# Block sums of the second weights from SBUF, and one load of values per chunk

## The chip, the cores and the metric

The kernel runs on one core of a Trainium2 chip. The metric is the device time of one execution in microseconds, from a few executions of the same program; the profiled execution is one more, and its span (first to last instruction) is what the rows of the trace are measured in.

## The reference

Three parts follow each other: local attention, a first feed-forward part with a layer norm, and a second, wider feed-forward part. All of it is float32, and the first two weight matrices and the two of the second part come in as 64-bit floats.

```
for each chunk of 32 tokens (B=4, H=8, S=768, D=64):        # attention
    keys, values = 8 memory rows + tokens from 16 before the chunk to 8 after it
    out = softmax(q @ keys.T / 8) @ values
x = out as [3072, 512]
h = x @ moe_w_in [512, 1024]; s = h * softmax(h)            # first part
x = ((s - mean) / sqrt(var + 1e-6) * g_ln) @ moe_w_out [1024, 512]
h = x @ moe2_w_in [512, 2048]                               # second part
out = (h * clip(h + 3, 0, 6) / 6) @ moe2_w_out [2048, 512]
```

## The kernel before

The 3072 tokens are 24 tiles of 128. The kernel is written as lists of names, and the order of the names is the order of the instructions on each engine; no scheduler moves them. `FIRST` is the way in (tiles 0 to 8 of the attention, the conversion of the first part's weights). `BODY` is one step of a loop over m = 8 to 23 and handles several tiles at once at different depths: it loads q, k and v for tiles m+6, m+7 and m+3, makes scores for m+3, applies probabilities to values for m+1 (`v_p`), multiplies by moe_w_in for m (`m1`), and by moe_w_out for a pair of earlier tiles (`m2`). m = 7 is written out at the end of `FIRST` (entries with @). `LAST` is the way into the second part; after it come only that part's products. "Step m" below is the pass of `BODY` for that m.

While the steps run, two more things are done beside them, for use in the second part. First, the 32 blocks of moe2 weights (16 of moe2_w_in, 16 of moe2_w_out, two in each step) are turned from 64-bit into 32-bit floats. The line of work for one block is: `load_w2` (SyncE, a transfer of 512 KB into z0 or z1, L431 and L434), `w2_abs` (ScalarE, L309), `w2_hold` (GpSimd, L316), `w2_bits` 0, 1, 2 (VectorE, L320, L323, L326), and `w2_store` (SyncE, to w2d in DRAM, L449). A z tile holds one block, so the next load of its kind can start only when `w2_bits` 2 has read it. Secondly, the second part multiplies by blocks in a scheme with fewer products, for which it needs sums and differences of blocks. For these `load_pair` (L852) reads two stored blocks back from DRAM into `pair`, `sum_pair` makes four block sums of 128x256 on GpSimd (L859, L861), and `sums_out` (L872) stores them.

```
def load_pair(kind, j):
    raw["pair"] = T("xal", [P, 2, 2, 256], name="pair")
    SP.dma_start(out=raw["pair"], in_=w2d[kind][j]...)
```

Every transfer of the loop is issued by SyncE (SP in the rows, SPq where its queue waits), in the order of the lists. `load_v` issues 8 loads a tile (4 chunks by 2 groups of 4 heads, L278); for the first two tiles of each batch, which are loaded in steps 9, 10, 15 and 16, it issues 8 more for the memory rows (L274).

A PSUM bank named h is shared: `m1` fills it, `ln_max` (DVE L710), `ln_exp` (ACT L716) and `ln_solu` (DVE L727) read it, then `qk_go` (PE L547) takes it for transposes of q and k, ScalarE copies those out to kT and qc (L303), and only then can the next `m1` (PE L701) write it. On ScalarE these copies stand around `w2_abs`, on VectorE `ln_max` and `ln_solu` stand among the `w2_bits`.

Of the kernel before, what the change touches and what calls it, by code (L numbers as in the profile page):

```python
# [61 lines left out]
    wo_bits:3,0 wo_hi:4 wo_lo:1 wo_bits:3,1 wo_hi:2 m2:0,3 wo_lo:2 ln_sq:3 wo_bits:3,2 wo_hi:5 m1:5,0 ln_var:3
    wo_hi:3 s_max:7 m2:0,0 wo_lo:4 wo_lo:5 wo_lo:3 m2:0,1 q_e:8,0,A ln_pow:3 wo_bits:7,2 x_h:6,1 ln_norm:3 ln_p:3,1
    ln_sq:4 ln_p:3,0 m2:0,4 load_w2:0 k_e:8,1,D wo_hi:7 ln_max:5 wo_lo:7 q_e:8,1,A load_w2:1 wo_hi:6 wo_lo:6 s_sub:7
    ln_exp:5 x_l:6,1 m2:0,2 s_exp:7 w2_abs:1,A m2:0,5 m1:6,0 w2_abs:0,A ln_den:5 ln_solu:5 m2_e:0,0 w2_hold:1,D
    ln_mean:5 ln_h:3,1,0 ln_sq:5 ln_var:4 ln_h:3,0,1 ln_l:3,0,1 s_sum:7 ln_var:5 ln_pow:5 w2_bits:1,0 s_rec:7
    s_norm:7,D ln_l:3,1,0 m1:6,1 m2_e:0,1 ln_norm:5 p_p:7 m2:0,6 p_e:7,0,A ln_pow:4 ln_norm:4 w2_hold:0,D s_p:8
    load_k:10 p_e:7,1,A ln_max:6 ln_exp:6 m2_s:0,0 load_v:7 v_p:7 load_k:9 ln_p:4,1 ln_p:4,0 m2:0,7 w2_bits:1,1
    w2_bits:1,2 x_h:7,0 x_l:7,0 load_w2:3 ln_den:6 m2:0,9 ln_solu:6 ln_mean:6 ln_h:4,1,0 ln_l:4,1,0 w2_store:1
    w2_abs:3,A load_q:9 s_max:8 m2:0,8 m2_s:0,1 ln_sq:6 ln_var:6 s_sub:8 s_exp:8 s_sum:8 m2:0,10 m2:0,11 ln_p:5,0  # L70
    m2_e:0,2 load_v:9 s_rec:8 ln_h:4,0,0 load_q:10 ln_pow:6 m2_s:0,2 ln_l:4,0,0 q_p:9 m2_e:0,3 ln_h:5,0,0 ln_l:5,0,0
    q_go:9,A ln_p:5,1 ln_h:5,1,0 s_norm:8,P ln_norm:6 k_mem:9,D block_p:9 load_k:11 load_q:11 block_p:10 block_e:9,A
    block_e:10,A load_k:12 ln_l:5,1,0 @m2:0 late_turn @s_p_at:6 @qk_p_at:6 @k_e_at:6,3 @k_e_at:6,0 @k_e_at:6,1
    @q_e_at:6 @k_e_at:6,2 p_p:8 p_e:8,1,A @m2:2 w2_hold:3,P p_e:8,0,A @s_max @s_sub @s_exp load_q:12 @w2_bits:0,0
    @w2_bits:0,1 @m1:0 @w2_bits:0,2 @w2_store:0 m2_s:0,3 load_k:13 @load_w2:0 @w2_abs:0 @w2_bits:1,0 @w2_bits:1,1
    @w2_bits:1,2 @w2_store:1 @m1:1 @ln_p @load_w2:1 @s_sum @s_norm @ln:max @ln_h:0 @w2_hold:0 @ln:exp @ln:den @v_p
# [11 lines left out]
    ln_l:1 p_e:0  # L88
# [72 lines left out]
def tile_chunked_attention_solu_hardswish(  # L161
# [1343 lines left out]
```

## Time and profile before

| | us |
|---|---|
| median of 3 executions | 897.89 |
| lowest and highest | 896.66 and 899.6 |
| the profiled execution | 896.33 |
| its span, first to last instruction | 894.5 |

The profiled execution is 1.56 us under the median, and its span 1.83 us under its own time. Busy shares are of the span. TensorE's clock has two levels, 1.2 and 2.4 GHz; the column PEclk gives the granted share of the higher one.

### The profile page before, as it was taken

To read this page: it belongs to the slowest core of one execution; us is meant where nothing else is said; L and a number is where in the kernel's file an instruction comes from. 1 tells how busy PE (TensorE), PEld (TensorE's weight loads), DVE (VectorE), ACT (ScalarE), POOL (GpSimd) and SP (SyncE) were. 2 spreads that over 40 slices of the span, in tenths; PEclk is the share of its full clock that TensorE was granted. 3 is DMA by queue.
4 is the path that set the end of the run, shared out by engine and by line. 5 is a ranking of instruction groups with operands and counts; after the bars stand their busy time and mean duration, and the time that the engine had idled before them with its cause. 6 is when DMAs were issued, how large, how long until landed. Compare 5 with 4: busy or idle time off the path is not lost.

```text
span 894.5 us, 22089 instructions
## 1 busy us (share of the span) xinstructions
PE 856.8 (96%) x8526; PEld 808.1 (90%) x8526; DVE 735.8 (82%) x1510; ACT 478.5 (53%) x946; POOL 252.6 (28%) x226
## 2 busy tenths in 40 slices
PE   9999999988999899998989999999999999999997
PEld 7777887977898789898989999999999999999997
DVE  7889976856687687756588999898899999999985
ACT  5888654645655555444363545545665444444542
POOL 4336214543645556534331111112430000000000
PEclk9999999999999999999999999999999999999999
DMA  8782476768897787654564456354877544444441
GB/s 229 194 267 65 110 181 201 226 186 244 270 242 215 243 229 232 186 177 147 188 209 175 156 198 235 123 211 175 266 259 233 196 153 132 139 156 136 138 142 60
DMA packets 185257, 168.34 MB, mean 188 GB/s; under 512 B 106816, under 2 KB 155456, under 8 KB 185152
## 3 DMA queue, kind: packets, MB, share of 16 engines
q1 hardware_dynamic: 184864, 166.67, 59.9%
q8 instruction: 67, 1.10, 0.5%
q14 instruction: 38, 0.31, 0.1%
q10 hardware_dynamic: 288, 0.26, 0.1%
HBM read 108.17 MB, written 58.72 MB: 187 GB/s over the span
## 4 chain that ended last, share of the span: by engine, by line
PE 65%; DVE 11%; DMA 11%; ACT 4%; issue 4%; SPq 3%; POOL 2%; DVEq 0%; POOLq 0%; ACTq 0%
PE acc L1104 22%; PE acc L1017 20%; PE m L805 8%; PE h L701 7%; DMA w2raw<-in_moe_w_out_dram 3%; DMA w2raw<-in_moe_w_in_dram 3%; PE tp L670 1%; SPq L278 1%; DMA pair<-w2d 1%; DVE f_s L1055 1%; DVE lst L710 1%; PE idle L1172 1%; DMA f_qb<-sums 1%; PE s L540 1%; DMA g<-f_s 1%
## 5 line engine op out<-in xcount | busy, mean ns | idle before, releaser
L805 PE MATMUL m<-lnh,wo 128*128 128x256 f32 (+1 forms) x704 | 144.2, 295 | 2.9 <-DVE x2o L815 2.8
L805 PEld LDWEIGHTS m<-lnh,wo 128*128 128x128 f32 x704 | 114.5, 190 | 5.5 <-DVE x2o L815 3.1
L701 PE MATMUL h<-w,xh 128*128 128x512 f32 x336 | 107.3, 401 | 6.0 <-ACT kT L303 6.0
L1052 ACT ACTIVATE f_s<-f_e,constants 128x512 f32<-128x512 f32 x96 | 67.9, 720 | 81.7 <-DVE f_e L1045 63.8
L805 PE MATMUL m<-lnl,wo 128*128 128x256 f32 (+1 forms) x352 | 102.2, 291 | 0.0
L701 PEld LDWEIGHTS h<-w,xh 128*128 128x128 f32 x336 | 62.0, 190 | 19.4 <-ACT kT L303 7.5
L1055 DVE SCALAR_TENSOR_TENSOR f_s<-f_s,f_e 128x512 f32<-128x512 f32 x96 | 69.9, 736 | 0.9 <-ACT f_s L1052 0.9
L316 POOL TENSOR_SCALAR w2t<-w2t 128x512 f32<-128x512 f32 x30 | 58.4, 1946 | 38.5 <-ACT w2t L309 32.0
L805 PEld LDWEIGHTS m<-lnl,wo 128*128 128x128 f32 x352 | 67.0, 190 | 0.7
L701 PE MATMUL h<-w,xl 128*128 128x512 f32 x168 | 66.2, 394 | 0.3 <-POOL xl L346 0.3
L815 DVE COPY x2o<-m 128x512 f32<-128x512 f32 (+1 forms) x26 | 16.6, 646 | 35.1 <-PE m L805 35.1
L716 ACT ACTIVATE e<-h,lst 128x1024 f32<-128x1024 f32 x24 | 26.8, 1116 | 30.3 <-DVE lst L710 30.3
L906 ACT ACTIVATE b_qb<-f_kn 128x384 fp32r<-128x384 f32 (+1 forms) x48 | 27.7, 577 | 28.2 <-DVE f_kn L1083 15.7
L309 ACT ACTIVATE w2t<-w2raw 128x512 f32<-128x512 f32 x32 | 21.4, 671 | 35.2 <-DMA w2raw<-in_moe_w_in_dram 15.5
L701 PEld LDWEIGHTS h<-w,xl 128*128 128x128 f32 x168 | 32.0, 190 | 7.7 <-POOL xl L346 0.7
L1041 DVE TENSOR_TENSOR f_e<-acc,f_e 128x512 f32<-128x512 f32 x48 | 32.9, 685 | 5.5 <-PE acc L1017 4.5
L346 DVE TENSOR_TENSOR lnl<-tp,lnh 128x512 fp32r<-128x512 f32 x41 | 28.1, 686 | 11.1 <-ACT lnh L342 11.1
L710 DVE TENSOR_REDUCE lst<-h 128x1 f32<-128x1024 f32 x24 | 29.2, 1215 | 7.1 <-PE h L701 7.0
L1049 DVE TENSOR_TENSOR f_e<-acc,f_e 128x512 f32<-128x512 f32 x48 | 32.9, 686 | 1.1 <-PE acc L1017 0.2
L644 POOL TENSOR_TENSOR pn<-pe,ast 128x512 f32<-128x512 f32 x21 | 22.2, 1058 | 36.6 <-DVE ast L640 19.8
L303 ACT ACTIVATE pb<-tp 64x512 f32<-64x512 f32 x47 | 27.9, 593 | 7.7 <-PE tp L652 4.0
L727 DVE SCALAR_TENSOR_TENSOR so<-h,lst,e 128x1024 f32<-128x1024 f32 x24 | 30.8, 1283 | 0.8
(465 smaller groups left out, 2547.9 us busy)
## 6 DMA issues: line engine op xcount, KB each, us to landing
g<-f_s SPq DMA_DIRECT2D x48, 512.0 KB
v<-in_v_dram SPq DMA_DIRECT2D x176, 56.0 KB
w2raw<-in_moe_w_in_dram SPq DMA_DIRECT2D x16, 512.0 KB
w2raw<-in_moe_w_out_dram SPq DMA_DIRECT2D x16, 512.0 KB
w2d<-w2t SPq DMA_DIRECT2D x32, 256.0 KB
pair<-w2d SPq DMA_DIRECT2D x16, 512.0 KB
sums<-sums SPq DMA_DIRECT2D x16, 512.0 KB
q_raw<-in_q_dram SPq DMA_DIRECT2D x24, 256.0 KB
```

The source lines that it names most:

```text
L316: ENG[eng].tensor_scalar(out=tf, in0=tf, scalar1=U_LO, scalar2=U_HI, op0=ALU.max, op1=ALU.min)
L346: (POOL if far else DVE).tensor_tensor(lo, r, hi.bitcast(F32), ALU.subtract)
L701: PE.matmul(h[:, f], a[:, kt], w[kt][:, f * 512:(f + 1) * 512], start=n == 0, stop=n == 3 * NKT - 1)
L710: DVE.tensor_reduce(st_t[i][:, 2:3], h_t[i].rearrange("p a b -> p (a b)"), axis=AX.X, op=ALU.max, negate=True)
L727: DVE.scalar_tensor_tensor(out=so_t[i], in0=h_t.pop(i).rearrange("p a b -> p (a b)"), scalar=st[:, 5:6], in1=e_t[i], op0=ALU.mult, op1=ALU ...
L805: PE.matmul(acc, w[fc // 2][:, fc % 2, dc * P:(dc + 1) * P], a[:, fc], start=fresh and k == 0, stop=k == len(todo) - 1, skip_group_check=True)
L1017: PE.matmul(o, w[wl][:, c * P:(c + 1) * P], x[xl][:, c], start=m == 0 and half == 0, stop=m == 5, skip_group_check=True)
L1041: DVE.tensor_tensor(c_of(n)[1], bank(n % 2, 2), wide(c_of(n)[0][:, 1]), ALU.add)
L1049: DVE.tensor_tensor(c, bank(n % 2, 3), c, ALU.add)
L1052: ACT.activation(out=g_of(n)[k], in_=c_of(n)[k], func=AF.Relu, bias=three, scale=1.0)
L1055: DVE.scalar_tensor_tensor(out=g_of(n)[k], in0=g_of(n)[k], scalar=6.0, in1=c_of(n)[k], op0=ALU.min, op1=ALU.mult)
L1104: PE.matmul(bank(t % 2, k)[:, half], g[al][:, G_BLOCK[p]], b_op[j, p][bl], start=j == 0 and m == 0 and half == 0, stop=j == NU - 1 and m = ...
```

## The change

`load_pair` is gone. The blocks of moe2_w_in now stay in the tile xal (two at a time), those of moe2_w_out in t0 and t1 by block number, and `sum_pair` reads them there, as soon as both of a pair are converted; the sums start at step 7 with moe2_w_out and end at step 22. `w2_store` leaves out the quarter of the blocks' columns that only the sums needed from DRAM (every other store is 256 columns instead of 512). In `BODY`, `sum_pair` moves from the start of the step to behind the last `w2_bits`, and `sums_out` from between the two weight loads to behind both.

`load_v` takes all 8 heads of a chunk in one transfer: 4 loads a tile instead of 8, and 4 for the memory rows instead of 8. The tiles of values and probabilities are laid out to fit, and with them the order in which `s_p`, `s_go`, `p_q` and `v_p` write their blocks and where `s_edge` masks; the number and shapes of their matmuls stay. The lists `FIRST` and `LAST` are written in another order.

```diff
 BODY = """
-    sum_pair m1:1 m1:0 w2_bits:0,0 m2:0 s_max w2_bits:0,1 w2_bits:1,0 s_sub w2_bits:0,2 ln:max w2_bits:1,1 s_exp
-    w2_bits:1,2 m2:1 ln:exp w2_store:0 v_p ln:den ln:solu s_sum s_p load_w2:0 x_h qk_p k_e:0 ln:mean sums_out q_e
-    w2_store:1 k_e:1 w2_abs:0 k_e:3 s_norm k_mem w2_hold:0 ln_p m2:2 m2:3 load_w2:1 ln:sq load_v x_l turn m2_e k_e:2
-    p_p ln:var load_k ln_h:0 load_pair ln:pow ln_l:0 ln_h:1 ln:norm w2_abs:1 p_e:1 m2_s load_q ahead w2_hold:1
+    m1:1 m1:0 w2_bits:0,0 m2:0 s_max w2_bits:0,1 w2_bits:1,0 s_sub w2_bits:0,2 ln:max w2_bits:1,1 s_exp w2_bits:1,2
+    sum_pair m2:1 ln:exp w2_store:0 v_p ln:den ln:solu s_sum s_p load_w2:0 x_h qk_p k_e:0 ln:mean q_e w2_store:1
+    k_e:1 w2_abs:0 k_e:3 s_norm k_mem w2_hold:0 ln_p m2:2 m2:3 load_w2:1 sums_out ln:sq load_v x_l turn m2_e k_e:2
...
     def load_v(i):
...
+        for c in range(4):
+            x, r0 = c % 2, 64 * (c // 2)
+            if i % TPB < 2 and (i >= 2 or x == 0):
+                SP.dma_start(out=dst[r0:r0 + NM, x], in_=mem_v[b].rearrange("h m d -> m h d"))
...
+            SP.dma_start(out=dst[r0 + NM + lo - s0:r0 + NM + hi - s0, x],
+                         in_=v[b, :, lo:hi, :].rearrange("h t d -> t h d"))
...
     def w2_abs(u, eng):
-        raw["w2t", u] = T(f"t{u % 2}", [P, 512], U32, "w2t")
+        f, part = divmod(u, 2)
+        if part:
+            raw["w2t", u] = T(f"t{f % 2}", [P, 512], U32, "w2t")
+        else:
+            if f % 2 == 0:
+                raw["w2p"] = T("xal", [P, 2, 512], U32, "w2t")
+            raw["w2t", u] = raw["w2p"][:, f % 2]
...
     def sum_pair(kind, j):
-        w = raw["pair"]
+        w = [raw["w2t", 4 * j + 2 * f + kind].bitcast(F32).rearrange("p (h c) -> p h c", h=2) for f in range(2)]
...
         def pair_of(m):
-            return 1 - m % 2, (m - 8) // 2
+            return m % 2, (m - STEADY) // 2
```

SyncE, from the first weight load of step 9 on, before (names: w2raw are the 64-bit blocks, w2d and sums_0_139 DRAM, w2t the converted blocks, kn the keys):

```order
L431 DMA w2raw<-in_moe_w_in_dram 128x4x128
L872 DMA sums_0_139<-sums 128x1024
L449 DMA w2d_1_124<-w2t 128x512
L434 DMA w2raw<-in_moe_w_out_dram 128x512
L274 DMA v_134<-in_mem_v_dram 8x4x64 x4
L278 DMA v_134<-in_v_dram 40x4x64
L278 DMA v_134<-in_v_dram 56x4x64 x3
L274 DMA v_134<-in_mem_v_dram 8x4x64 x4
L278 DMA v_134<-in_v_dram 40x4x64
L278 DMA v_134<-in_v_dram 56x4x64 x3
L256 DMA kn_131<-in_k_dram 128x8x64
L852 DMA pair<-w2d_1_124 128x1024
```

The same place of the changed kernel:

```order
L426 DMA w2raw<-in_moe_w_in_dram 128x4x128
L451 DMA w2d_1_124<-w2t 128x512
L429 DMA w2raw<-in_moe_w_out_dram 128x512
L861 DMA sums_1_148<-sums 128x1024
L272 DMA v_134<-in_mem_v_dram 8x8x64
L275 DMA v_134<-in_v_dram 40x8x64
L272 DMA v_134<-in_mem_v_dram 8x8x64
L275 DMA v_134<-in_v_dram 56x8x64
L272 DMA v_134<-in_mem_v_dram 8x8x64
L275 DMA v_134<-in_v_dram 56x8x64
L272 DMA v_134<-in_mem_v_dram 8x8x64
L275 DMA v_134<-in_v_dram 56x8x64
```

The store of the sums has moved behind the second weight load, the sixteen loads of values are eight, and no load of a pair follows the keys.

GpSimd in step 9, with what each instruction waits for in brackets (DMAHW is a transfer's landing), before:

```order
L861 TENSOR_TENSOR sums<-pair 128x256 [waits DMAHW4_49,DMAHW0_49,Pool_49]
L859 TENSOR_TENSOR sums<-sums,pair 128x256 [waits Pool_49]
L859 TENSOR_TENSOR sums<-pair 128x256
L859 TENSOR_TENSOR sums<-pair,sums 128x256 [waits Pool_49]
L644 TENSOR_TENSOR pn<-pe,ast 128x512 [waits DVE_49,PE_49,Activation_49]
L316 TENSOR_SCALAR w2t<-w2t 128x512 [waits DMAHW7_49,Activation_49]
```

And of the changed kernel, where one pair later stands in its place:

```order
L848 TENSOR_TENSOR sums<-w2t 128x256 [waits DMAHW6_49]
L848 TENSOR_TENSOR sums<-w2t,sums 128x256 [waits DVE_49,Pool_49]
L848 TENSOR_TENSOR sums<-w2t 128x256
L848 TENSOR_TENSOR sums<-w2t,sums 128x256 [waits Pool_49]
L642 TENSOR_TENSOR pn<-pe,ast 128x512 [waits DVE_49,PE_49,Activation_49]
L311 TENSOR_SCALAR w2t<-w2t 128x512 [waits Activation_49]
```

The four sums keep their place in GpSimd's order, ahead of the attention's `s_norm` (pn) and the next block's `w2_hold`; what they wait for is VectorE (the last `w2_bits`) instead of the landing of a pair.

## Rows read from the trace of the kernel before

**Rows 1.** The page: span, and busy time of each engine.

```profile
span 894.5 us, 22089 instructions
PE 856.8 (96%) x8526; PEld 808.1 (90%) x8526; DVE 735.8 (82%) x1510; ACT 478.5 (53%) x946; POOL 252.6 (28%) x226
```

**Rows 2.** Busy by stretch, cut where `v_p` starts: length, PE, PEld, DVE, ACT, POOL, PEclk, DMA, GB/s.

```profile
60.00:137.08 77.08, 71.55 (x655) 61.46 (x653) 66.09 (x110) 52.52 (x110) 27.72 (x23) 0.98 0.53 136
137.08:168.59 31.51, 29.52 (x395) 26.39 (x393) 24.63 (x41) 19.27 (x43) 13.60 (x11) 1.00 0.73 208
168.59:183.36 14.77, 14.77 (x205) 13.45 (x204) 10.31 (x21) 7.64 (x17) 8.21 (x8) 1.00 0.57 178
183.36:222.17 38.81, 31.89 (x409) 28.37 (x409) 23.89 (x43) 18.73 (x41) 16.42 (x16) 0.96 0.77 226
222.17:253.78 31.61, 29.75 (x409) 26.78 (x408) 23.78 (x41) 18.39 (x43) 17.82 (x17) 1.00 0.92 263
253.78:283.95 30.17, 29.62 (x409) 26.94 (x409) 21.98 (x44) 16.68 (x37) 16.41 (x16) 1.00 0.73 214
283.95:321.16 37.21, 31.84 (x410) 27.99 (x409) 24.78 (x43) 19.40 (x43) 19.33 (x20) 0.95 0.86 255
321.16:350.87 29.71, 29.48 (x409) 26.75 (x409) 23.84 (x41) 17.32 (x37) 17.21 (x15) 1.00 0.74 223
350.87:379.14 28.27, 27.76 (x313) 25.02 (x312) 21.76 (x38) 13.91 (x28) 17.71 (x18) 1.00 0.65 195
```

**Rows 3.** Timeline, SyncE's queue, step 9 into step 10: start, length, issues.

```profile
173.66 0.42 SPq L434 DMA_DIRECT2D w2raw<-in_moe_w_out_dram  x1
175.65 2.94 SPq L278 DMA_DIRECT2D v<-in_v_dram  x4
...
182.21 0.58 SPq L852 DMA_DIRECT2D pair<-w2d  x1
...
184.81 0.45 SPq L431 DMA_DIRECT2D w2raw<-in_moe_w_in_dram  x1
```

**Rows 4.** Timeline, 181 to 194 us; in brackets the idle time ahead and its releaser.

```profile
181.07 0.43 DVE L320 TENSOR_SCALAR w2t<-w2t 128x512 uint32<-128x512 uint32 x1 [2.14 <-POOL w2t L316]
...
186.93 0.47 PE L547 MATMUL qk<-ident,q_raw 64*128 64x64 f32 x8 [1.62 <-issue]
...
191.22 0.67 ACT L309 ACTIVATE w2t<-w2raw 128x512 f32<-128x512 f32 x1 [2.15 <-DMA w2raw<-in_moe_w_in_dram]
...
193.34 0.73 PE L701 MATMUL h<-w,xh 128*128 128x512 f32 x2 [0.99 <-ACT kT L303]
```

**Rows 5.** Timeline, SyncE's queue around 253.78, where `v_p` of step 14 starts.

```profile
251.30 0.38 SPq L431 DMA_DIRECT2D w2raw<-in_moe_w_in_dram  x1
...
257.61 0.67 SPq L434 DMA_DIRECT2D w2raw<-in_moe_w_out_dram  x1
```

**Rows 6.** Waits of SyncE's queue, whole span: us in total, times, longest.

```profile
SPq L872 <- POOL sums L859: 62.4, 16, 5.3
...
SPq L278 <- DMA w2raw<-in_moe_w_out_dram: 10.0, 13, 1.5
```

**Rows 7.** Timeline around 253.78: the end of the block conversion, `ln_solu`, `qk_go`, `w2_abs`.

```profile
252.93 0.69 DVE L326 SCALAR_TENSOR_TENSOR w2t<-w2raw,w2t 128x512 uint32<-128x512 uint32 x1
...
254.00 1.28 DVE L727 SCALAR_TENSOR_TENSOR so<-h,lst,e 128x1024 f32<-128x1024 f32 x1
...
255.65 0.47 PE L547 MATMUL qk<-ident,q_raw 64*128 64x64 f32 x8
...
257.68 0.67 ACT L309 ACTIVATE w2t<-w2raw 128x512 f32<-128x512 f32 x1
```

**Rows 8.** Timeline around 320 us: VectorE's last `w2_bits`, a block sum on GpSimd.

```profile
320.49 1.11 DVE L326 SCALAR_TENSOR_TENSOR w2t<-w2raw,w2t 128x512 uint32<-128x512 uint32 x1
...
319.87 1.19 POOL L859 TENSOR_TENSOR sums<-pair 128x256 f32<-128x256 f32 x1
```

**Rows 9.** Timeline, TensorE in `LAST`.

```profile
409.30 0.44 PE L805 MATMUL m<-lnh,wo 128*128 128x384 f32 x1 [2.80 <-DVE x2o L815]
```

More of the change, by code (lines that the diff above doesn't have):

```diff
@@ L62 @@
[L62 to L76, printed above, removed]
@@ new lines @@
+    ln_var:5 s_sum:7 s_rec:7 load_w2:0 w2_abs:0,A m2_e:0,0 m1:6,1 ln_var:4 ln_pow:5 ln_norm:5 ln_pow:4 w2_hold:1,D
+    ln_h:3,1,0 s_norm:7,D p_p:7 w2_bits:1,0 load_k:9 ln_norm:4 load_v:7 ln_l:3,1,0 m2:0,6 ln_p:4,1 m2_s:0,0
+    p_e:7,1,A ln_max:6 p_e:7,0,A ln_h:4,1,0 s_p:8 w2_bits:1,1 w2_bits:1,2 v_p:7 x_h:7,0 load_w2:3 load_k:10
+    w2_store:1 ln_p:4,0 ln_l:4,1,0 ln_p:5,0 k_mem:9,D m2:0,7 w2_hold:0,D ln_exp:6 ln_den:6 ln_solu:6 ln_mean:6
+    s_max:8 ln_sq:6 m2:0,8 ln_var:6 x_l:7,0 m2:0,9 m2:0,10 load_q:9 s_sub:8 s_exp:8 m2_e:0,2 ln_h:4,0,0 s_sum:8
@@ L80 @@
+    @w2_store:1 @sum_pair @sums_out @s_sum @s_norm @load_w2:1 @m1:0 @m1:1 @ln:max @w2_abs:0 @ln_p @ln:exp @ln:den
+    @s_p @ln:solu @v_p @x_h @ln:mean @m2:3 @m2:1 @ln_h:0 @ln_l:0 @m2_e @qk_p @p_p @load_q @ln_h:1 @ln_l:1 @k_e:0
+    @k_e:3 @x_l @q_e @k_e:1 @k_e:2 @load_k @k_mem @ln:sq @ln:var @w2_hold:0 @ln:pow @w2_abs:1 @p_e:1 @w2_hold:1
+    @ln:norm @w2_store:0 @p_e:0 @m2_s @load_v
 """
 BODY = """
-    sum_pair m1:1 m1:0 w2_bits:0,0 m2:0 s_max w2_bits:0,1 w2_bits:1,0 s_sub w2_bits:0,2 ln:max w2_bits:1,1 s_exp
@@ L89 @@
+    k_e:1 w2_abs:0 k_e:3 s_norm k_mem w2_hold:0 ln_p m2:2 m2:3 load_w2:1 sums_out ln:sq load_v x_l turn m2_e k_e:2
+    p_p ln:var load_k ln_h:0 ln:pow ln_l:0 ln_h:1 ln:norm w2_abs:1 p_e:1 m2_s load_q ahead w2_hold:1 ln_l:1 p_e:0
 """
@@ L228, in tile_chunked_attention_solu_hardswish @@
     km = [km[:, 0], km[:, 1]]
-    vx = [T(f"v{i}", [P, 4, 4, D]) for i in range(2)]
+    vx = [T(f"v{i}", [P, 2, H, D]) for i in range(2)]
     qb = T("qb", [P, 4, 4, 2, C])
-    pb = T("pb", [P, 4, 4, 2, C])
+    pb = T("pb", [P, 2, H, 2, C])
     kT = [T("kT", [P, 4, 4, NK])] * 2
@@ L448, in w2_store @@
         f, part = divmod(u, 2)
-        SP.dma_start(out=w2d[part][f // 2][:, f % 2], in_=raw["w2t", u].bitcast(F32))
+        kept = slice(0 if f % 2 == part else 256 * (1 - part), 512 if f % 2 == part else 512 - 256 * part)
+        SP.dma_start(out=w2d[part][f // 2][:, f % 2, kept], in_=raw["w2t", u].bitcast(F32)[:, kept])
     def load_g():
@@ L598, in s_edge @@
     def s_edge(i):
-        first, last = (slice(0, C), slice(3 * C, P)) if i >= BLOCKS else (slice(0, P), slice(0, P))
-        if i % TPB == 0:
-            t = sc_t[i][first] if i >= BLOCKS else sc_t[i][:, 0]
-            for t in [t[:, y] for y in range(2)] if i >= BLOCKS else [t]:
-                DVE.memset(t[..., NM:NM + LC], NEG)
-        if i % TPB == TPB - 1:
-            t = sc_t[i][last] if i >= BLOCKS else sc_t[i][:, 3]
-            for t in [t[:, y] for y in range(2)] if i >= BLOCKS else [t]:
-                DVE.memset(t[..., NK - RC:NK], NEG)
+        for edge, n, keys in ((0, 0, slice(NM, NM + LC)), (TPB - 1, 3, slice(NK - RC, NK))):
+            if i % TPB == edge and i >= BLOCKS:
+                for y in range(2):
+                    DVE.memset(sc_t[i][:, y, n, keys], NEG)
+            elif i % TPB == edge:
+                DVE.memset(sc_t[i][:, n // 2, :, n % 2, keys], NEG)
     def s_max(i):
```

203 lines of the change are left out of this document (93 added, 110 removed).

## Prediction

> **What bounds the kernel now.** I began with the page: TensorE is busy for 96% of the span, the next engine, VectorE, for 82% [rows 1]. So the time is TensorE's work plus the places where it stands still or runs at its lower clock, and no stage can give more than those. The view by stretch, cut where `v_p` starts, shows where they are in the loop [rows 2]. The stretch from 168.59 is one step in which TensorE never stops: 14.77 us long, 14.77 busy. I call that a full step. Thirteen of the fifteen steps between 137.08 and 379.14 have the same work; the last two (28.27 together) have less. What each stretch has over full steps (two steps are 29.54):
>
> - 137.08 to 168.59: 31.51, over by 1.97
> - 183.36 to 222.17: 38.81, over by 9.27, at a granted clock of 0.96
> - 222.17 to 253.78: 31.61, over by 2.07
> - 253.78 to 283.95: 30.17, over by 0.63
> - 283.95 to 321.16: 37.21, over by 7.67, at 0.95
> - 321.16 to 350.87: 29.71, over by 0.17
>
> Together 21.8 us. Two stretches have 16.94 of it; they follow steps 9, 10, 15 and 16, in which memory rows are loaded as well. The entries lie at the two ends of this: the stretch from 60 to 137.08, in which TensorE is idle for 77.08 - 71.55 = 5.5, and a stop of 2.80 in `LAST` [rows 2, 9].
>
> Next I asked what TensorE waits for in the first bad stretch, and went back from there. The transposes of q and k start at 186.93 after 1.62 idle, and the next `m1` at 193.34 after 0.99, released by a copy of ScalarE [rows 4]. The first is VectorE's lateness: it had stood 2.14 before 181.07 until GpSimd had held a block [rows 4]. That block's load was issued at 173.66 [rows 3], 7.4 us before. The second is ScalarE, which stood 2.15 before 191.22 for the load of the other block [rows 4], with copies out of bank h queued behind it. That load was issued at 184.81 [rows 3], 1.45 after the cut at 183.36, while in a full step it goes out at 251.30, 2.48 before the cut at 253.78 [rows 5]: 3.9 us late.
>
> Both lates are made in SyncE's queue. After 173.66 it issues sixteen loads of values and one of keys before the pair at 182.21 [rows 3], 18 steps from issue to issue in 8.55 us, 0.475 each. Four of them alone took 2.94 [rows 3], and the waits say why: SyncE stood at these loads 13 times, 10.0 us in all, for the load of moe2_w_out to land [rows 6]. The other wait is `sums_out`: 16 times, 62.4 us [rows 6]. Behind it stands the load of moe2_w_out, which goes out at 257.61 although the block's z tile was free at 252.93 + 0.69 = 253.62 [rows 5, 7]. So a ring runs through the queue: load of a pair, block sums, `sums_out`, weight load, loads of values, next load of a pair.
>
> **The change part by part.**
>
> *The pair's load and the wait for it.* The sums need no transfer any more, and `sums_out` stands behind the weight load. The load of moe2_w_out can then go out at about 253.7 in place of 257.61, 3.9 us earlier; the stop that it ends was 2.14 [rows 4, 5, 7], so it is hidden with 1.8 to spare. `sums_out` still waits for GpSimd, but what stands behind it now (values, keys, x2d, q) is needed a step or more later. That is the edit that I cost at nothing; its cover is the time until the next weight load, some 10 us, and it is gone if values take longer than that.
>
> *Values.* In steps 9, 10, 15 and 16 eight issues fewer: 8 x 0.475 = 3.8 us, about the 3.9 by which 184.81 is late. The bound on the other side: a transfer of twice the bytes takes twice as long to issue, and nothing is saved. I take the first, since the issue waits here for landings of other transfers and not for its own bytes [rows 6]; in the other case the load at 184.81 still gains the pair's 0.58 and the earlier start.
>
> *What this gives in TensorE's time.* The four bad steps take 76.02. I expect them at 14.95, between the pairs that have no memory rows (30.17 / 2 = 15.09 and 29.71 / 2 = 14.86): 59.8, a gain of 16.2. The lower clock goes with the stops: both stretches below 1.00 are those that stop. The two steps behind the first bad pair are over because VectorE catches up; 31.61 to 29.9, 1.7. The first two hang on the way in as well; half of 1.97 is 1.0.
>
> *Where the sums now lie.* In even steps both blocks are ready after `w2_bits` 2 of moe2_w_in, ahead of the last two `w2_bits` of the other block, so these and GpSimd's sums run together. Rows 8 show such a pair: 1.11 us instead of the 0.69 of rows 7. Two instructions, 0.42 each: up to 0.85 a step on VectorE ahead of `ln_solu`, which ends at 255.28 where the transposes start at 255.65 [rows 7], 0.37 ahead. So between 0 and 8 x 0.85 = 6.8 us in eight even steps. The step cut at 321.16 has this overlap already and is a full one [rows 2, 8]; I take 0.15 each, 1.2 us. The Trainium skill ("GPSIMD Engine Reference", Specifications) says that GpSimd shares its SBUF interfaces with VectorE and contends with instructions there that have two SBUF inputs, as these have; the rows agree. By the rule alone, with no regard to the slack, the cost would be the upper bound.
>
> *v_p, s_go, p_q, masks, stores:* the same matmuls in another order, and stores half as long; 0, bounds 0.3 either way by their small share of a full step.
>
> *The entries.* Other orders of the same instructions. They can give back at most the 5.5 before 137.08 and the 2.80 with its slow clock; they can lose as much. Nothing in the trace prefers a sign: 0, with 3 either way.
>
> Sum: 16.2 + 1.7 + 1.0 - 1.2 = 17.7. The profiled execution took 896.33, so 878.6; the median of the executions shown is 1.56 above it (897.89), so 880.2. Forecast 880.
>
> **The rivals.**
>
> *Transfers, not the queue's order* (0.18). If the 512 KB loads land late however early they are issued, half of the 17.9 of the four bad and two later steps stays: 889. For it: the DMA share is 0.92 from 222.17 and 0.86 from 283.95 [rows 2]. Against it: the worst stretch has only 0.77, the one with 0.92 is over by 2.07 alone, and 512 KB of each step's traffic go.
>
> *Sums against VectorE* (0.10). The overlap costs its bound in every even step, 6.8 instead of 1.2: 886. For it: rows 8. Against it: the full step at 321.16. This is the Trainium skill's rule at its full price.
>
> *Nothing is won* (0.04). The weight loads turn out to be held by something else, such as the z tile freed later, and the new program keeps the old steps: 897. Against it: 253.62 to 257.61 [rows 5, 7].
>
> *Slower* (0.05). In every even step ScalarE's `w2_abs` must now write into xal, which the sums of that step still read; if they are late, ScalarE stops with the copies out of bank h behind it. A quiet ScalarE gets there at 257.68 [rows 7]; by my estimate the sums can start when the first block is done, one `w2_bits` 1 and 2 and a piece of the attention ahead of 252.93, some 2 us; four at up to 1.19 each [rows 8] end near 255.7, 2 us before it. It costs TensorE only what exceeds that; to eat 17.7 and end 0.3% above before (900.6) it must exceed it by (17.7 + 2.7) / 8 = 2.6 us in each of the eight, a sum 4.6 us later than I put it.
>
> **How the numbers follow.** Forecast 0.63 (its own range 875 to 886 by the entries and the bound of the values), transfers 0.18, VectorE 0.10, nothing 0.04, slower 0.05. The range reaches from 872 (all 21.8 of the loop and most of the entries) to 891, which takes in the first three; outside lie 0.09 and their tails. About 0.3% is what a measurement of this kernel can tell from no change. Faster 0.91, same 0.04, slower 0.05.
>
> **What would show it.** Right: steps of 14.7 to 15.1 throughout, also where memory rows are loaded; no granted clock under 1.00 between 137 and 380; the load of moe2_w_out within 0.5 us of the last `w2_bits`; SyncE's wait for GpSimd still there, with no engine behind it. `w2_bits` near 1.1 us in even steps, without a stop of the transposes. Wrong would be: `w2_abs` still stopped for the loads of weights (transfers); the transposes stopped behind `ln_solu` in every second step (VectorE); `w2_abs` stopped for GpSimd (the slower case); or a stop before 137 or after 380 that was not there, which would move the sum by the entries that I set to 0.

## The result, and the profile after

The changed kernel takes 869.4 us, the median of 4 executions (868.13 to 870.86), beside 898.5 for the kernel before (896.66 to 899.6): a ratio of 0.968, with a 95% interval of 0.965 to 0.970. That is 29.1 us faster. The forecast was 880, 17.7 faster, in a range from 872 to 891. So the direction was right and the time lies below the range. The profiled execution took 870.14, with a span of 868.3.

The page of the changed kernel, span and engines; the counterpart of [rows 1]:

```profile
span 868.3 us, 21875 instructions
PE 847.9 (98%) x8526; PEld 803.2 (92%) x8526; DVE 739.5 (85%) x1510; ACT 476.6 (55%) x946; POOL 256.3 (30%) x226
```

TensorE runs as many matmuls, 8526, and is busy 8.9 us less (it was 856.8); of the 26.2 us of span the other 17.3 were idle. The view by stretch, cut at the same starts of `v_p` as [rows 2], with the same columns:

```profile
60.00:136.15 76.15, 70.69 (x718) 60.61 (x717) 66.39 (x110) 52.91 (x111) 30.08 (x27) 1.00 0.53 133
136.15:166.50 30.35, 28.63 (x334) 25.67 (x329) 23.28 (x40) 18.42 (x41) 14.50 (x12) 1.00 0.72 193
166.50:181.18 14.68, 14.68 (x206) 13.36 (x206) 11.76 (x24) 9.01 (x21) 10.53 (x11) 1.00 0.80 232
181.18:210.60 29.42, 29.41 (x409) 26.71 (x409) 23.36 (x41) 17.73 (x40) 18.01 (x17) 1.00 0.81 223
210.60:240.03 29.43, 29.42 (x410) 26.72 (x409) 23.36 (x41) 17.70 (x40) 18.07 (x17) 1.00 0.81 220
...
269.56:298.98 29.42, 29.41 (x409) 26.71 (x409) 23.36 (x41) 17.72 (x40) 18.01 (x17) 1.00 0.80 216
298.98:328.41 29.43, 29.42 (x410) 26.72 (x409) 21.82 (x39) 15.81 (x34) 15.93 (x15) 1.00 0.61 174
328.41:357.06 28.65, 28.09 (x314) 25.13 (x314) 22.65 (x40) 15.08 (x31) 17.63 (x18) 1.00 0.52 157
```

From 166.50 to 328.41 no step is over 14.85 us, and TensorE is idle for no more than 0.01 us in any of the stretches shown there. The two stretches that were 38.81 and 37.21 in [rows 2] are 29.42 each, at a granted clock of 1.00; TensorE was busy there for 31.89 and 31.84 and is for 29.41, so the lower clock of before is seen in the busy time as well. The loop (from `v_p` of step 7 to `v_p` of step 22) took 379.14 - 137.08 = 242.1 us and takes 357.06 - 136.15 = 220.9. That is 21.2 of the 26.2. Of the other 5.0, 0.9 lies ahead of the loop (137.08 to 136.15) and 4.1 behind it (from step 22's `v_p` to the end of the span 515.36, now 511.24). The first cut does not part the same work, though: in the changed `FIRST` the scores of step 7 (`s_p`) stand ahead of its `v_p`, in the list of before behind it.

```profile
135.36 0.86 PE L540 MATMUL s<-kT,qc 64*32 64x64 f32 x64
```

That is 0.86 us of TensorE's work, and it accounts for the 395 matmuls in the stretch from 137.08 [rows 2] beside the 334 in the one from 136.15. From `v_p` of step 8 on (153.17 and 151.13) both kernels have the same work: 225.97 and 205.93, 20.0 less, with 2.0 of the 26.2 ahead of it.

SyncE's queue in the same place as [rows 3], steps 9 and 10, in the timeline:

```profile
178.69 0.39 SPq L426 DMA_DIRECT2D w2raw<-in_moe_w_in_dram  x1
181.65 0.34 SPq L451 DMA_DIRECT2D w2d<-w2t  x1
182.09 0.38 SPq L429 DMA_DIRECT2D w2raw<-in_moe_w_out_dram  x1
182.56 0.41 SPq L861 DMA_DIRECT2D sums<-sums  x1
183.06 1.16 SPq L272 DMA_DIRECT2D v<-in_mem_v_dram  x1
...
189.99 0.40 SPq L255 DMA_DIRECT2D kn<-in_k_dram  x1
...
194.01 0.39 SPq L426 DMA_DIRECT2D w2raw<-in_moe_w_in_dram  x1
```

The load of moe2_w_out goes out ahead of the sums' store. Eight loads of values take from 183.06 to 189.99, and the next load of moe2_w_in leaves at 194.01, after a pause: the queue waits for the work, not the work for the queue. The waits of that queue say the same (us in total, times, longest):

```profile
SPq L451 <- DVE w2t L321: 53.5, 16, 6.4
...
SPq L861 <- POOL sums L848: 14.2, 9, 2.7
...
SPq L275 <- DMA sums<-sums: 3.3, 2, 2.2
SPq L272 <- DMA w2raw<-in_moe_w_out_dram: 1.9, 3, 1.1
```

The store of the sums waits 14.2 us in all where it waited 62.4 [rows 6], and the loads of values wait 1.9 instead of 10.0 for moe2_w_out. The longest wait of the loop is now that of the blocks' stores for VectorE's last `w2_bits`, 53.5.

### The profile page after: what moved, and what is told of

The parts are those of the page before. It is cut to its first block, busy times and chain, and to the rows that moved or that the text cites. A ratio compares the mean times of both kernels' runs of the same rounds, so it can differ in the third digit from the quotient of the medians.

```text
span 868.3 us, 21875 instructions
## 1 busy us (share of the span) xinstructions
PE 847.9 (98%) x8526; PEld 803.2 (92%) x8526; DVE 739.5 (85%) x1510; ACT 476.6 (55%) x946; POOL 256.3 (30%) x226
## 4 chain that ended last, share of the span: by engine, by line
PE 80%; DVE 11%; DMA 2%; issue 2%; ACT 2%; POOL 1%; DVEq 0%; POOLq 0%; ACTq 0%; SPq 0%
PE acc L1093 26%; PE acc L1006 21%; PE m L798 13%; PE h L694 10%; PE tp L668 2%; PE s L540 1%; DVE f_s L1044 1%; PE qk L547 1%; PE idle L1161 1%; PE tp L547 1%; DVE so L720 1%; PE sc L595 1%; DMA woraw<-in_moe_w_out_dram 1%; DVE lst L703 1%; PE tp L583 1%
## 5 line engine op out<-in xcount | busy, mean ns | idle before, releaser
L1044 DVE SCALAR_TENSOR_TENSOR f_s<-f_s,f_e 128x512 f32<-128x512 f32 x96 | 72.0, 758 | 0.7 <-ACT f_s L1041 0.7
L311 POOL TENSOR_SCALAR w2t<-w2t 128x512 f32<-128x512 f32 x30 | 59.8, 1992 | 20.8 <-ACT w2t L304 20.8
L627 ACT ACTIVATE pe<-pe 128x512 f32<-128x512 f32 x24 | 15.2, 632 | 39.6 <-DVE pe L622 38.2
L848 POOL TENSOR_TENSOR sums<-w2t,sums 128x256 f32<-128x256 f32 x24 | 20.8, 865 | 33.5 <-DVE w2t L321 33.5
```

Source lines behind the costliest of these rows:

```text
L311: ENG[eng].tensor_scalar(out=tf, in0=tf, scalar1=U_LO, scalar2=U_HI, op0=ALU.max, op1=ALU.min)
L1044: DVE.scalar_tensor_tensor(out=g_of(n)[k], in0=g_of(n)[k], scalar=6.0, in1=c_of(n)[k], op0=ALU.min, op1=ALU.mult)
```

## The experiments

All times are medians. Each ratio is to the kernel before on the same chip, with its 95% interval. "Loop" is the time from `v_p` of step 7 to `v_p` of step 22, from the starts of the two groups in the profiled execution's timeline, and "from 8" the time from `v_p` of step 8. Each is read from one execution, which lies up to 2.4 us from its kernel's median (884.13 with only the store moved, 885.48 with only the loads of values changed, 875.28 with only those undone). Three things can be set apart in SyncE's loop, and eight kernels hold all their combinations:

| values, loads a chunk | store of sums | sums made from | time | ratio | loop | from 8 |
|---|---|---|---|---|---|---|
| 2 | between | reloaded pair (before) | 898.5 | 1 | 242.1 | 226.0 |
| 1 | between | reloaded pair | 883.65 | 0.986 (0.982 to 0.990) | 233.8 | 215.6 |
| 2 | behind | reloaded pair | 886.53 | 0.989 (0.985 to 0.994) | 228.3 | 211.6 |
| 1 | behind | reloaded pair | 872.22 | 0.972 (0.969 to 0.974) | 221.9 | 205.1 |
| 2 | between | SBUF | 881.77 | 0.983 (0.980 to 0.985) | 231.4 | 216.4 |
| 1 | between | SBUF | 880.19 | 0.980 (0.978 to 0.982) | 233.7 | 218.7 |
| 2 | behind | SBUF | 873.06 | 0.974 (0.969 to 0.978) | 226.5 | 211.5 |
| 1 | behind | SBUF (changed) | 869.4 | 0.968 (0.965 to 0.970) | 220.9 | 205.9 |

The lists `FIRST` and `LAST` are those of before in the first four rows and those of the change in the last four, which also store the blocks without the quarter that only the sums needed. The list `FIRST` alone makes some 0.9 of a difference in "loop", by the scores of step 7; between the first four rows and the last four, "from 8" is the one to compare.

**The store of the sums behind the weight loads, alone.** An edit of the kernel before:

```diff
-    ... x_h qk_p k_e:0 ln:mean sums_out q_e
-    w2_store:1 k_e:1 w2_abs:0 k_e:3 s_norm k_mem w2_hold:0 ln_p m2:2 m2:3 load_w2:1 ln:sq load_v ...
+    ... x_h qk_p k_e:0 ln:mean q_e
+    w2_store:1 k_e:1 w2_abs:0 k_e:3 s_norm k_mem w2_hold:0 ln_p m2:2 m2:3 load_w2:1 sums_out ln:sq load_v ...
```

> The kernel before with one entry moved: the store of the sums stands behind both weight loads instead of between them. The pair is still read back, and values still take 8 or 16 loads. My queue theory: the load of moe2_w_out no longer waits for GpSimd and goes out about 3.9 us earlier, so the first of the two late blocks in a bad step is cured; the wait itself still stands ahead of the sixteen loads of values, so the load of moe2_w_in after them stays late. About half of the 16.9 us of the four bad steps: 890, between 886 and 894. Rival, the reload of the pair and its traffic are what cost: within 2 us of before, 897 to 900. Rival, the wait only moves (values and keys now late): slower than before.

886.53 (882.27 to 891.74), loop 228.3: inside what the queue theory gave, outside both rivals. One moved entry of a list takes 13.8 us out of the profiled loop; by the medians of the two kernels on that chip it is worth 11.3 (897.83 to 886.53).

**One load of values per chunk, alone.** The kernel before with `load_v`, `s_go`, `s_edge`, `p_q`, `s_p` and `v_p` of the change:

```diff
-                    in_=v[b, h0:h0 + 4, lo:hi, :].rearrange("h t d -> t h d"),
+                         in_=v[b, :, lo:hi, :].rearrange("h t d -> t h d"))
```

> The kernel before with the change of the values alone: one load per chunk for all heads, with the layouts that go with it; the pair is read back, and all three lists are those of before. My queue theory: in the four steps with memory rows eight issues at 0.475 us fewer, so the load of moe2_w_in goes out 3.8 us earlier and the second late block is cured; the first stays. About half of 16.9: 890, between 886 and 894. Rival, a load of twice the bytes takes the queue twice as long: within 2 us of before. Rival, the two lates are one chain and either cure is enough: 882 to 885.

883.65 (878.43 to 886.9), loop 233.8. The rival that nothing is saved falls. The median lies under the range of the queue theory and inside that of the third case, 882 to 885. The profiled loop speaks against that case: 8.2 of 21.2 (10.4 of 20.0 from step 8), so this cure alone leaves about half.

**Both of these, with the pair still reloaded.** The two edits above in one kernel.

> The kernel before with the two edits together that were made apart: one load of values per chunk, and the store of the sums behind both weight loads. The pair is still stored whole, read back and summed from there; FIRST and LAST are those of before. In the profiles the first edit alone took 8.2 us off the loop's 242.0 (step 7 to 22, by v_p), the second alone 13.8, the whole change 21.1. Theory, SyncE's queue is all of the gain in the loop: its loop is within 1.5 us of the changed kernel's 220.9, and with the list LAST of before (some 3 us) the time is 871 to 876. Rival, the sums from SBUF (no reload, no wait for it) hold a part of their own: the loop stays at 225 or more, 878 to 884.

872.22 (870.51 to 874.75), loop 221.9: within 1.0 of the changed kernel's. This decides the question. The sums still come from a pair that is stored, read back and waited for, and 20.2 of the loop's 21.2 us are there. The 1.0 that is left is the cut at step 7 and not the sums: from step 8 on this kernel takes 205.1 and the changed one 205.9, and the changed kernel with the old `FIRST` (below) has a loop of 221.95. By time, the changed kernel with the old `LAST` (below) takes 872.51, as much as this one. Two stretches of it, each two steps, with the columns of [rows 2]:

```profile
182.20:211.54 29.34, 29.34 (x409) 26.70 (x408) 22.87 (x40) 17.68 (x40) 18.37 (x18) 1.00 0.94 284
211.54:241.19 29.65, 29.43 (x410) 26.73 (x409) 23.47 (x41) 17.69 (x40) 19.94 (x19) 1.00 0.97 264
```

The first has memory rows, and TensorE is busy in all of its 29.34, with the DMA engines busy for 94% of the time.

**The sums from SBUF, without the two.** The changed kernel with two loads of 4 heads per chunk in the steps (those of the memory rows likewise), and `sums_out` between the weight loads:

```diff
-            SP.dma_start(out=dst[r0 + NM + lo - s0:r0 + NM + hi - s0, x],
-                         in_=v[b, :, lo:hi, :].rearrange("h t d -> t h d"))
+            for h in (slice(0, 4), slice(4, 8)) if i > BLOCKS else (slice(0, 8),):
+                SP.dma_start(out=dst[r0 + NM + lo - s0:r0 + NM + hi - s0, x, h],
+                             in_=v[b, h, lo:hi, :].rearrange("h t d -> t h d"))
-    ... ln:mean q_e w2_store:1 k_e:1 ... load_w2:1 sums_out ln:sq load_v ...
+    ... ln:mean sums_out q_e w2_store:1 k_e:1 ... load_w2:1 ln:sq load_v ...
```

> The changed kernel with both edits of the queue undone: values in two loads of 4 heads in the steps, and the store of the sums between the weight loads. What is left of the change are the sums from SBUF, the shorter stores and the lists FIRST and LAST. Theory, SyncE's queue is all of the gain in the loop: about its loop of before, 238 to 243 (steps with memory rows at 18 and over), and with LAST's some 3 us the time is 885 to 895. Rival, the sums from SBUF hold half of the gain or more: 230 or less, 881 and below (the store's place alone, undone, gave 880).

881.77 (880.08 to 885.72), loop 231.4: better than the theory's 885 to 895, and not as good as the rival's bound. Alone, the sums from SBUF take 10.7 us out of the loop (9.6 from step 8). On top of the other two they take nothing that these runs can show. The three are not three gains: each shortens the same ring of waits (8.2, 13.8 and 10.7 add to 32.7, and all together give 21.2).

**The store between the weight loads again.** The second half of the last diff alone, in the changed kernel.

> The changed kernel with the store of the sums between the two weight loads again, as before the change. My prediction costed its place as the reason that moe2_w_out was 3.9 us late. In the changed kernel's trace the sums of an even step end at about the time when that load goes out, those of an odd step 1.8 us behind it. If so, the load is held by at most 2.2 us in eight steps, about what it had in hand: 869 to 873. Rival, the place of the store alone carries half of the loop's gain: 879 or more.

880.19 (877.64 to 881.73), loop 233.7: the rival, which I had put at 879 or more. What happens is in the timeline, steps 9 and 10 of this run (in brackets the idle time ahead and its releaser):

```profile
168.21 0.74 POOL L848 TENSOR_TENSOR sums<-w2t,sums 128x256 f32<-128x256 f32 x1
...
168.97 0.34 SPq L861 DMA_DIRECT2D sums<-sums  x1
169.41 1.88 SPq L451 DMA_DIRECT2D w2d<-w2t  x1
171.37 0.38 SPq L429 DMA_DIRECT2D w2raw<-in_moe_w_out_dram  x1
...
175.95 0.67 ACT L304 ACTIVATE w2t<-w2raw 128x512 f32<-128x512 f32 x1 [2.31 <-issue]
...
178.66 0.43 DVE L315 TENSOR_SCALAR w2t<-w2t 128x512 uint32<-128x512 uint32 x1 [1.88 <-POOL w2t L311]
...
185.16 0.46 PE L547 MATMUL qk<-ident,q_raw 64*128 64x64 f32 x8 [1.95 <-issue]
```

The last sum of an odd step ends at 168.95, and only then the store of the sums, the store of the block and the load of moe2_w_out go out, at 171.37. In the changed kernel that load left at 167.05 (`v_p` of the step started 0.1 apart in the two):

```profile
167.05 0.39 SPq L429 DMA_DIRECT2D w2raw<-in_moe_w_out_dram  x1
```

I had seen only the 1.8 us by which the sums end behind the load, and not the store of the block between them, which stood 1.88 itself. Then the chain of the prediction follows: ScalarE stands 2.31 (the profile names no releaser), GpSimd holds the block late, VectorE stands 1.88, `ln_solu` is late and the transposes stop for 1.95. The step also pays a second time, by the clock (windows of steps 9 and 10, columns as before):

```profile
166.39:181.27 14.88, 14.74 (x205) 13.38 (x205) 10.36 (x22) 7.93 (x20) 8.31 (x9) 1.00 0.74 210
181.27:199.59 18.32, 16.37 (x206) 15.01 (x206) 13.85 (x23) 10.00 (x22) 9.50 (x8) 0.91 0.72 190
```

Of the 18.32 - 14.67 = 3.65 us over a full step, 1.95 is the stop, and 16.37 - 14.67 = 1.70 is longer matmuls at a mean clock of 0.91.

**Sixteen loads of values again.** The first half of the same diff alone, in the changed kernel.

> The changed kernel with the loads of values in the steps cut in two again (4 heads each): 8 a tile, 16 in the four steps with memory rows; everything else as changed. Queue theory: in the trace of the changed kernel SyncE is through with a bad step's loads some 2 us before the next weight load may go; eight more issues at 0.475 make that 1.8 us late, less what the next conversion has in hand: 1 to 2 us in each of the four steps, 870 to 877. Rival, the number of issues carries most of the gain: half of the 21 us or more comes back, 880 and over. Rival, without the reload and its wait the issues are free: 869 to 870, and no step over 14.9.

873.06 (869.9 to 875.59), loop 226.5: the queue theory's case. The six times lie in two groups, 869.9 to 870.84 and 875.28 to 875.59, and the profiled execution, 875.28, is of the second; in the first the time is about that of the changed kernel, so the loss below is that of every second execution or so. In the trace only two of the four steps that were bad before are long (16.82 and 19.01). Ahead of the first the queue is at values from 183.88 until 193.84, where 183.06 to 189.99 were enough for half as many: 9.96 - 6.93 = 3.0 us for eight issues. The next load of moe2_w_in, the copy that waits for it, and the next `m1`:

```profile
196.45 0.52 SPq L428 DMA_DIRECT2D w2raw<-in_moe_w_in_dram  x1
...
202.51 0.68 ACT L306 ACTIVATE w2t<-w2raw 128x512 f32<-128x512 f32 x1 [1.85 <-DMA w2raw<-in_moe_w_in_dram]
...
204.65 0.73 PE L696 MATMUL h<-w,xh 128*128 128x512 f32 x2 [1.57 <-ACT kT L300]
```

The load leaves 2.4 later than in the changed kernel (194.01), and TensorE stops for 1.57 behind ScalarE's copies. This is the second late of the prediction, by itself.

**The pair's traffic without anyone waiting.** The changed kernel, with whole stores and a copy of each pair to a spare place in DRAM:

```diff
+    def load_pair(kind, j):
+        SP.dma_start(out=pair_d, in_=w2d[kind][j])
-        SP.dma_start(out=w2d[part][f // 2][:, f % 2, kept], in_=raw["w2t", u].bitcast(F32)[:, kept])
+        SP.dma_start(out=w2d[part][f // 2][:, f % 2], in_=raw["w2t", u].bitcast(F32))
-    p_p ln:var load_k ln_h:0 ln:pow ...
+    p_p ln:var load_k ln_h:0 load_pair ln:pow ...
```

> The changed kernel with the traffic of before put back: the stores of blocks are whole again, and at the old place of the pair's load its two blocks are copied, 512 KB, from DRAM to a spare place in DRAM that nothing reads. No engine waits for the copy. Queue theory: only the issue comes back, about 0.6 us a step with 1 to 2 us free in the queue: 869 to 872. Rival, the transfers' share of the DMA engines is what made the loads late: half or more of the 21 us of the loop comes back, 880 or more.

868.96 (866.6 to 872.13), ratio 0.970 (0.967 to 0.974), loop 220.6: no difference. 30 us of the loop in this run:

```profile
210.00:240.00 30.00, 29.99 (x415) 27.29 (x414) 23.94 (x42) 17.71 (x41) 18.63 (x17) 1.00 0.95 272
```

The DMA share is 0.95 instead of the changed kernel's 0.81, and TensorE is busy for 29.99 of 30. The rival "transfers, not the queue's order" is out.

**The list `LAST` of before** in the changed kernel (the diff is that list, reversed).

> The changed kernel with the list LAST of before; the rest as changed. Between the two profiles the stretch from the last v_p to the end of TensorE's work is 4.7 us shorter in the changed kernel. If the order of LAST is the cause, these come back: 874, between 873 and 876, with TensorE's stops around the products of the first blocks (three of 0.74 to 0.88 before). Rival, they come from the steps ahead of it (sums and blocks are in DRAM earlier, the queue is freer): within 1 us of the changed kernel.

872.51 (872.15 to 875.02), ratio 0.972 (0.970 to 0.975), 3.1 above the changed kernel's median; from step 22's `v_p` to the end 513.16. Over the profiles, the five kernels with the old list take 512.6 to 515.8 for that stretch (mean 514.2), the seven with the new one and nothing else moved in it 509.9 to 512.8 (mean 510.9). So the order of `LAST` is worth some 3 us. In that stretch TensorE is idle for 12.4 us before, for 12.8 in this run and for 10.2 in the changed kernel. Where it lies is in the timeline of TensorE, first in the kernel before:

```profile
454.66 0.98 PE L1017 MATMUL acc<-b_kT,b_ll 128*128 128x256 f32 x6 [0.88 <-DVE f_e L1038]
...
457.24 0.98 PE L1017 MATMUL acc<-b_q,b_ll 128*128 128x256 f32 x6 [0.74 <-DVE f_e L1045]
...
459.75 0.97 PE L1017 MATMUL acc<-b_t,b_ll 128*128 128x256 f32 x6 [0.82 <-DVE f_e L1049]
...
488.64 0.98 PE L1017 MATMUL acc<-b_wo,b_xah 128*128 128x256 f32 x6 [0.47 <-DVE f_e L1045]
```

In this run, with the same list:

```profile
408.55 0.93 PE L1006 MATMUL acc<-b_q,b_wb 128*128 128x256 f32 x6 [1.50 <-DVE x2o L808]
...
433.45 0.98 PE L1006 MATMUL acc<-b_q,b_ll 128*128 128x256 f32 x6 [0.75 <-DVE f_e L1034]
...
436.02 0.98 PE L1006 MATMUL acc<-b_t,b_ll 128*128 128x256 f32 x6 [0.91 <-DVE f_e L1038]
```

And in the changed kernel, all of its stops between 400 and 500 us:

```profile
435.45 0.74 PE L1006 MATMUL acc<-b_km,b_wo 128*128 128x256 f32 x4 [0.18 <-POOL b_wo L898]
...
446.17 3.00 PE L1006 MATMUL acc<-b_wo,b_wb 128*128 128x256 f32 x24 [0.62 <-DVE f_e L1027]
```

**The list `FIRST` of before** in the changed kernel, with the pair's load taken out and the first sums put in:

```diff
-    ... @k_e:1 @k_e:3 @load_pair @p_p ...
+    ... @w2_bits:1,2 @sum_pair @w2_store:1 ... @load_w2:1 @sums_out ... @k_e:1 @k_e:3 @p_p ...
```

> The changed kernel with the list FIRST of before, the load of the pair taken out and the first sums and their store put in at the places that BODY has them; the rest as changed. Between the two profiles v_p of step 7 comes 1.1 us earlier, and the next steps are 1.1 us shorter together. If that is the order of FIRST: 1 to 2.5 us slower than the changed kernel, 870.5 to 872. Rival, the list also decides in what order the blocks and the queue enter the loop, and old stops return in steps 7 to 10: 4 us or more, 873 and over. Rival, no difference: within 0.6.

867.66 (866.82 to 868.27), ratio 0.966 (0.964 to 0.968): 1.7 under the changed kernel's first median and 0.6 under that of its repetition below, so not slower, and nearest to the third case. `v_p` of step 7 even starts earlier, at 133.97 against 136.15, but step 7 then takes 17.13 instead of 14.99, and step 8 starts at 151.10 and 151.14. In the kernel before it started at 153.17, in the three others that keep the reload at 152.72 to 154.85, and in the ten without it at 150.06 to 152.55. So the 2 us up to step 8 are not the order of the list. That the reload is their cause is not shown: in step 7 it is issued behind `v_p`, while this run gains ahead of that (133.97 against 137.08 before) and not in step 7 itself (17.13 against 16.09), and among kernels of the same kind the starts differ by up to 2.5 us.

**The changed kernel again,** beside the runs of before that three other kernels shared.

> The changed kernel unaltered, on the same chip and beside the same runs of before as the others of this call, to give the size of the difference between repetitions: 867 to 871, its loop 220.9 within 0.5, the stretch from the last v_p to the end of TensorE's work 505.7 within 1.5.

868.3 (866.13 to 871.3), ratio 0.967 (0.965 to 0.970), loop 220.9 and 509.9 from step 22's `v_p` to the end. A repetition moves the median by 1 us and the last stretch by 1.4.

**The stop of 2.80 in `LAST`.** It stands in the changed kernel as it did in [rows 9], released by a copy out of PSUM on VectorE:

```profile
387.21 0.45 PE L798 MATMUL m<-lnh,wo 128*128 128x384 f32 x1 [2.80 <-DVE x2o L808]
```

Two runs move that copy (`m2_e:9,1`); the second, whose diff is shown, moves `x_lo:0,2` behind the other copy as well:

```diff
-    ... x_sum:0,2 m2:10,0 x_sum:0,4 m2:10,1 w_hi:1 w_lo:1 x_hi:0,5 w_lo:3
-    load_w:5 load_w:4 w_lo:2 x_hi:0,2 x_hi:0,6 x_lo:0,2 w_hi:4 m2:10,2 m2_e:10,0 m2_e:9,1 x_sum:0,3 ...
+    ... x_sum:0,2 m2:10,0 x_sum:0,4 m2_e:9,1 m2:10,1 w_hi:1 w_lo:1 x_hi:0,5 w_lo:3
+    load_w:5 load_w:4 w_lo:2 x_hi:0,2 x_hi:0,6 w_hi:4 m2:10,2 m2_e:10,0 x_lo:0,2 x_sum:0,3 ...
```

> The changed kernel with one entry of LAST moved: the copy of group 9's second bank out of PSUM goes ahead of the second piece of group 10's products instead of behind its third, so ahead of three splits of weights on VectorE. TensorE's stop of 2.80 at 384.5 waits for that copy, and the lower clock behind it (0.91 in the 20 us from 378) costs some 1.8 more. If the copy alone ends the stop: 2.8 to 4.6 us faster, 865 to 866.6. Rival, the next bank's copy, which stands in the same place, holds TensorE as long: within 1 us of the changed kernel.

867.74 (865.37 to 870.16), ratio 0.966 (0.964 to 0.969). The stop became two, of 0.79 and 1.12, because the copy of the other bank stood behind splits as well; the gain is below what I expected of it, and by times alone not told from the changed kernel.

> The changed kernel with two entries of LAST moved: the copy of group 9's second bank ahead of the second piece of group 10 (as in the run before, in which the stop of 2.80 became two of 0.79 and 1.12 and the clock of that place rose to its higher level), and the copy of group 10's first bank ahead of one split on VectorE that held it 0.6. 0.5 us less than that run: 1.7 to 3 us faster than the changed kernel, 866 to 868. Rival, TensorE waits next for what the split behind the copy feeds: no faster than the changed kernel.

866.31 (865.27 to 866.75), ratio 0.9645 (0.962 to 0.967), beside 0.967 (0.965 to 0.970) for the changed kernel in the same comparison: 2.0 us less by the medians, with intervals that still overlap. TensorE's stops in `LAST` in this run:

```profile
380.22 0.61 PE L798 MATMUL m<-lnh,wo 128*128 128x384 f32 x2 [0.78 <-DVE x2o L808]
...
383.92 0.45 PE L798 MATMUL m<-lnh,wo 128*128 128x384 f32 x1 [0.65 <-DVE x2o L808]
```

The stretch of 20 us around them (376 to 396) in the changed kernel:

```profile
376.00:396.00 20.00, 17.20 (x103) 16.88 (x102) 12.97 (x16) 8.63 (x15) 10.17 (x8) 0.91 0.40 129
```

And in this run:

```profile
376.00:396.00 20.00, 18.57 (x126) 17.93 (x125) 15.15 (x19) 9.62 (x18) 11.76 (x8) 1.00 0.41 137
```

1.4 us less idle, and 23 matmuls more in the same time: two short stops are not followed by the lower clock, the long one is. It has the lowest median of all the kernels here.

## Why the prediction was wrong

**The mechanism was right.** The marks that the prediction set are in the trace, but for step 8, which took 15.37: steps of 14.7 to 14.85 also where memory rows are loaded, a granted clock of 1.00 in every stretch up to step 22, the load of moe2_w_out at 240.94, 0.46 after the last `w2_bits` of its step (239.36 + 1.12). The two lates and the ring through SyncE's queue are shown by experiment, each by itself: the store's place, and the number of loads of values. What the prediction left open is settled too: the sums from SBUF, by which the change is named, add nothing to the loop that shows once the queue is mended.

**The terms of the loop** were 17.7 together and measured 21.2 in the profiles.

| step of the prediction | forecast | measured |
|---|---|---|
| four bad steps, 76.02 to 59.8 | 16.2 | 17.2 (29.42 + 29.42 = 58.8) |
| two steps behind the first pair, 31.61 | 1.7 | 2.2 (29.43) |
| the first two, 31.51 | 1.0 | 1.2 (30.35), 0.9 of it the scores moved ahead of the cut |
| sums beside `w2_bits` on VectorE | -1.2 | within the rows above, about 0.1 an even step |
| the other stretches | not counted | 0.6 |

The steps came out at 14.71, not the 14.95 that I took from stretches which still had small stops. The full step of [rows 2] was the better yardstick, and the full steps were there to be read.

**The sums against VectorE.** The overlap is there. The even step around 240 us in the changed kernel, timeline:

```profile
236.40 0.68 DVE L321 SCALAR_TENSOR_TENSOR w2t<-w2raw,w2t 128x512 uint32<-128x512 uint32 x1
...
239.36 1.12 DVE L321 SCALAR_TENSOR_TENSOR w2t<-w2raw,w2t 128x512 uint32<-128x512 uint32 x1
...
239.88 1.19 POOL L848 TENSOR_TENSOR sums<-w2t,sums 128x256 f32<-128x256 f32 x1
...
240.58 1.28 DVE L720 SCALAR_TENSOR_TENSOR so<-h,lst,e 128x1024 f32<-128x1024 f32 x1
...
240.94 0.38 SPq L429 DMA_DIRECT2D w2raw<-in_moe_w_out_dram  x1
...
241.98 0.47 PE L547 MATMUL qk<-ident,q_raw 64*128 64x64 f32 x8
```

`w2_bits` 2 takes 1.12 beside a sum that takes 1.19, and alone it takes 0.68 (at 236.40 in the same step). The Trainium skill ("GPSIMD Engine Reference", Specifications) says that GpSimd contends for the SBUF interfaces with VectorE's instructions of two SBUF inputs; the trace agrees, by 1.12 to 0.68. But TensorE hardly stops at the transposes (0.01 us): `ln_solu` ends at 241.86, 0.12 ahead of them. The even steps take 14.75 to 14.85 and the odd ones 14.67 or 14.68. So the overlap, which I costed at 0.15 an even step, takes 0.1 in most of them and 0.2 in one if it is all of that difference, and the slack hides the rest.

**The entries: the step that failed.** "0, with 3 either way", and "they can give back at most the 5.5 before 137.08 and the 2.80". The order of `LAST` gave some 3 us. It did not give them at the 2.80, which is still there. It gave them at stops around 455 and 488 us (0.88, 0.74, 0.82 and 0.47, with matmuls between them that came later as well), which the trace of before had and which I left out of the bound, because I looked for one long stop. The way in gave 0.9 up to step 7, or 1.8 with the scores on the same side of the cut, and 2.0 up to step 8. The experiment with the old `FIRST` rules out its order; what gave them stays open. In the profiles the entries are 5.0 of the 26.2 us by the cut at step 7, 6.2 by the one at step 8.

**The range.** Its low end was said to hold "all 21.8 of the loop and most of the entries". Counted out, 897.9 - 21.8 - 5.5 - 2.8 = 867.8, and 872 leaves more than four of these. It also left no room for the difference of single executions: I added 1.56 to come from the profiled execution of before to the median, and the profiled execution of the changed kernel lies 0.74 above its own, 2.3 together. These three make up the miss: 3.5 in the loop, 5.0 at the entries, 2.3 between executions, 10.8 together (880.2 - 869.4). With the cut at step 8 the first two are 2.3 and 6.2.

**What stays open.** With the sums from SBUF and the store between, halving the values' loads shortens the loop to 231.4 from 233.7, while the medians go the other way (881.77 and 880.19, with intervals that overlap). I can't tell these from one profile each. How the 3 us of `LAST` split between its stops was not tried either.

## What to carry to other kernels

Where one queue issues all transfers in a written order, look for the entry that waits for an engine and ask what stands behind it. Here one moved name took 13.8 of the profiled loop's 21.2 us (11.3 by the medians), and the elegant part of the change, data that need not be read back, showed no gain on top of the two edits of the queue. Several cures of one ring of waits don't add: test them in combination before you count them. Where two kernels are compared between two marks in the trace, count the work between the marks first: here a mark that one list had moved past 0.86 us of work looked like a gain of 1.0. And a bound on what a rewritten list can give must be the sum of all stops in its stretch, short ones too, not the longest one.

## What the hardware showed that I had not expected

The DMA engines were busy for 94 to 97% of two stretches of about 29.5 us each (the run with both queue edits and the pair reloaded), and TensorE was idle for 0.0 and 0.2 of them. A share of 0.92 in [rows 2] had made me give the transfers a chance of 0.18; here the share by itself did not show lateness.

The loads of values did not cost a fixed time each: eight took 6.93 us in step 10 of the changed kernel and sixteen of half the size 9.96. That is 0.87 and 0.62 an issue, waits included, and 0.38 for each of the eight more, beside the 0.475 that I read from the kernel before. In step 9 of the same two runs it is 5.97 and 7.56, 0.20 for each of the eight more.
